# Eighteen first adds of the softmax sums moved to GpSimd, the first batch's factors one place later, one more w_out unit inside the attention

## Chip, cores and metric

One core of one Trainium2 chip runs the whole program. The metric is the device time of one execution in microseconds, over several runs; a profiled execution supplies the trace. TensorE does the matrix products (PE, its weight loads PEld), VectorE (DVE), ScalarE (ACT) and GpSimd (POOL) the rest, and SyncE (SP) starts the DMAs.

## What is computed

Three stages follow each other, each on the output of the one before (B=4 batches, S=448 positions, D=768):

```python
scores = scale * q @ k.transpose            # 4 batches, 12 heads, 448 positions, 64 wide
scores = cap * np.tanh(scores / cap)
attn = softmax(scores) ; x = attn @ v       # heads side by side: (4, 448, 768)

w = softmax of the 2 largest of x @ w_gate  # 4 experts
for e in range(4):                          # causal attention of one head of 64
    out += w[e] * (softmax(mask(q_e @ k_e.T)) @ v_e @ wo[e])

h = gelu(out @ w_in)                        # 768 -> 1024; u, v = halves
v_s = w_sg @ (norm(v) * g_ln) + b_sg        # over positions
y = out + (u * v_s) @ w_out                 # 512 -> 768
```

w_in and w_out arrive as float64 and are split into float32 words in the kernel.

## The kernel before

The attention works on 24 pairs of heads, pair i = 6b + hp (`pairs`), one in each call of `slot(i, side)` (line 281); two more slots empty the pipe. The scores are held transposed, keys on the partitions. Keys 0 to 255 of both heads form the half h = 0, the rest h = 1. `scores(i, h)` (line 201) does the matmuls into PSUM `s`, then tanh (ScalarE, into `p`) and one exponential of the whole half (ScalarE, in place). No maximum is subtracted, since the scores are capped.

The softmax's sum over the keys is made in two steps. `add_up(i, h)` (line 226) adds blocks of keys on VectorE: for h = 0 it makes `pb` (128x896) as the sum of the two blocks of `p`, for h = 1 it adds the third block to `pb`, and in odd slots half a block to each of two `pb`. `sums(b, i)` (line 261) then sums over the partitions with `onehot` on TensorE, for two pairs at once, and VectorE copies or adds the result to `rs`. Its PSUM buffer is from the pool `ps_g`, three buffers that `values` in odd slots and the experts' products use too. Six pairs make a batch. Then `invert(b)` (line 273) takes the reciprocal of `rs`, stores it to DRAM (`rd`) and loads it back, spread over partitions (`rb`, the factors). `values(i)` (line 238) makes the unscaled output `po` from `p` and v (`vv`, `vl`), and `os` holds it in SBUF. `over_sums` (line 331) multiplies `os` by the factors, and `in_parts` (line 335) splits it into a rounded part `xh` and a rest `xl`, the input of the experts.

In slot i the order is: scores(i, 0), side "w", values(i-2), side "a1", the first add, scores(i, 1), side "p", the sums of two pairs in even slots, the second add, side "n". The sides carry other work. In slots 0 to 9 that is the conversion of w_in (`prepare_weights`, on VectorE, products on TensorE); from slot 10 on (`beside`, line 559) a table `PLAN` places the experts' steps of earlier batches, `queries_keys`, `values_chunk`, `gates`, `weigh`, `settle`, `turn`, `attend`. `normed(n, place)` (line 344) places the steps of the factors; its batch is that of slot n - 6. `settle` scales the experts' softmax on GpSimd, `turn` transposes it on TensorE, with copies `pt` by VectorE.

`w_out(k, i, ...)` (line 371) converts one of eight units of w_out: a DMA (`wuw`), six operations of `from64` on VectorE (`wum`), three on GpSimd, two DMAs to DRAM. The table `W_OUT` (line 554) names the slot of each unit; numbers of 26 and more stand for steps of `experts_end` (line 585), which does the rest of the experts after the attention, interleaved with the gMLP of earlier batches (`gsv`, `vg`, the norm).

Up to slot 25, program order is kept on TensorE, VectorE, ScalarE and GpSimd by `InOrder` and `pin` (lines 95 to 120). After that a scheduler orders the instructions by its own costs. The queue of SyncE, which issues the DMAs, is ordered by the scheduler throughout. All operations of VectorE, ScalarE and GpSimd carry line 105 in the profile, all matmuls line 120, transposes line 487.

Of the kernel before, what the change touches and what calls it, by code (L numbers as in the profile page):

```python
# [17 lines left out]
ALU = mybir.AluOpType  # L18
# [4 lines left out]
HP = H // 2  # L23
# [15 lines left out]
def drain(gen):  # L39
    for _ in gen:  # L40
        pass
# [32 lines left out]
def build(ctx: ExitStack, tc: tile.TileContext, a: dict):  # L74
# [4 lines left out]
    def rnd(eng, out, in_):  # L79

        if eng == "a":
            act.activation(out, in_, AF.Copy)
        elif eng == "v":
            dve.tensor_copy(out, in_)
        else:
            pool_e.tensor_scalar(out, in_, 1.0, 0.0, op0=ALU.mult, op1=ALU.add)
# [22 lines left out]
    act, dve, pool_e = InOrder(nc.scalar), InOrder(nc.vector), InOrder(nc.gpsimd)  # L109
# [14 lines left out]
    xp = ES(tc.tile_pool(name="xp", bufs=1, reuse_waits="tile"))  # L124
# [19 lines left out]
    def scale():  # L144
        nc.sync.dma_start(capt, a["cap"].to_broadcast([128, 1]))
        dve.memset(tsc, 0.0)
        act.activation(tsc, tsc, AF.Tanh)
        dve.reciprocal(tsc, capt)
        dve.tensor_scalar(tsc, tsc, 1.0 / math.sqrt(D), None, op0=ALU.mult)
# [25 lines left out]
    at = ah.enter_context(tc.tile_pool(name="at", bufs=2, side="right"))  # L175
# [7 lines left out]
    def load_qk(i):  # L183

        b, hp = pairs[i]
        qk_t[i] = [at.tile([128, S], F32, tag=t, name=f"{t}{i}", bufs=3) for t in ("qp", "kp")]
        nc.sync.dma_start(qk_t[i][1], a["kT"][b, :, hp, :])
        nc.sync.dma_start(qk_t[i][0], a["qT"][b, :, hp, :])

    def load_v(i):  # L190

        b, hp = pairs[i]
        vv = at.tile([128, 2, KT // 128, D], F32, tag="vv", name=f"vv{i}", bufs=3)
        nc.sync.dma_start(vv, a["v"][b, :, 2 * hp:2 * hp + 2])
        vl = None
        if hp % 2:
            vl = at.tile([128, 2, D], F32, tag="vl", name=f"vl{i}", bufs=2)
            nc.sync.dma_start(vl, a["vl"][b, hp // 2])
        v_t[i] = vv, vl

    def scores(i, h):


        last = h == 1 and i % 2 == 1
        n = 2 if h == 0 or last else 1
        p = at.tile([128, 2, n, S], F32, tag=("p0", "p1" if n == 1 else "p2")[h], name=f"p{i}_{h}", bufs=(3, 1)[h])
        pend[i] = (*pend.get(i, ()), p)
        for c2 in range(n):
            s = ps_s.tile([128, 2, 512], F32, tag="s", name=f"s{i}_{2 * h + c2}")
            for j in range(2):  # L210
                r = slice(64 * j, 64 * j + 64)
                if c2 and last:
                    for half in range(2):
                        qp, kp = qk_t[i - 1 + half]
                        mm(s[64 * half:64 * half + 64, j, :S], kp[r, KT:], qp[r, :], start=True, stop=True)
                else:
                    qp, kp = qk_t[i]
                    c = 2 * h + c2
                    mm(s[:, j, :S], kp[r, c * 128:(c + 1) * 128], qp[r, :], start=True, stop=True)
            act.activation(p[:, :, c2, :], s[:, :, :S], AF.Tanh, scale=tsc)  # L220
            yield 805.0


        act.activation(p, p, AF.Exp, scale=capt)

    def add_up(i, h):
        p = pend[i][h]
        if h == 0:
            pb = pbs[i] = at.tile([128, 2, S], F32, tag="pb", name=f"pb{i}", bufs=3)
            dve.tensor_tensor(pb, p[:, :, 0, :], p[:, :, 1, :], op=ALU.add)  # L230
            return
        dve.tensor_tensor(pbs[i], pbs[i], p[:, :, 0, :], op=ALU.add)
        if i % 2:
            for half in range(2):
                r, pb = slice(64 * half, 64 * half + 64), pbs[i - 1 + half]
                dve.tensor_tensor(pb[r], pb[r], p[r, :, 1, :], op=ALU.add)

    def values(i):

        vv, vl = v_t.pop(i)  # L240
        odd = i % 2
        po = po_t[i] = (ps_g if odd else ps_o).tile([128, 512], F32, tag="g" if odd else "po", name=f"po{i}")
        if odd:
            b, hp = pairs[i]
            p = pend[i][1]
            for half in range(2):
                r = slice(64 * half, 64 * half + 64)
                for j in range(2):
                    mm(po_t[i - 1 + half][64 * j:64 * j + 64, :S], vl[r, j, :], p[r, j, 1, :],
                       start=(half == 1), stop=(half == 0))  # L250
            os_t[b, hp // 2] = ao.tile([128, 2, S], F32, tag="os", name=f"os{i}", bufs=4)
            act.activation(os_t[b, hp // 2][:, 0, :], po_t.pop(i - 1)[:, :S], AF.Copy)
        for c in range(KT // 128):
            for j in range(2):
                mm(po[64 * j:64 * j + 64, :S], vv[:, j, c, :], pend[i][c // 2][:, j, c % 2, :],
                   start=(c == 0 and not odd), stop=(c == KT // 128 - 1 and odd == 1))
            yield 805.0
        if odd:
            act.activation(os_t[b, hp // 2][:, 1, :], po_t.pop(i)[:, :S], AF.Copy)
# [21 lines left out]
    def slot(i, side):  # L281

        here = i < len(pairs)
        if i == 0:
            load_qk(0)
            scale()
            load_w(0)
            load_qk(1)  # L290
        if i % 2 == 0 and i + 2 < len(pairs):
            load_qk(i + 2)
        if here:
            first = scores(i, 0)
            drain(islice(first, 2))
            side("a")
            drain(first)
        else:
            side("a")
        side("w")  # L300
        if i > 1:
            drain(values(i - 2))
        if here:
            load_v(i)
        side("a")
        if here:
            add_up(i, 0)
            drain(scores(i, 1))
            if i % 2 == 1 and i + 2 < len(pairs):
                load_qk(i + 2)  # L310
        side("p")
        if 0 < i <= len(pairs):
            b, hp = pairs[i - 1]
            if hp % 2 == 1:
                drain(sums(b, hp // 2))
        if here:
            add_up(i, 1)
        side("n")
# [16 lines left out]
    def in_parts(b, h2):  # L335

        if h2 == 0:
            X[b] = (xp.tile([128, KC, S], F32R, tag="xh", name=f"xh{b}"),
                    xp.tile([128, KC, S], F32R, tag="xl", name=f"xl{b}"))
        (xh, xl), x, o = X[b], os_t.pop((b, h2)), slice(2 * h2, 2 * h2 + 2)  # L340
        rnd("v", xh[:, o, :], x)
        rest("v", xl[:, o, :], x, xh[:, o, :])

    def normed(n, place):

        b = (n - 1) // HP - 1
        step = (n % HP, place)
        if n > B * HP + 4 or b < 0:
            return
        if step == (1, "a1"):  # L350
            invert(b)
        elif step == ((3, "w") if b else (2, "a1")):
            over_sums(b, 0)
            over_sums(b, 1)
            load_rb(b, 2)
        elif b == 0 and step == (3, "w"):
            in_parts(b, 0)
            in_parts(b, 1)
        elif b == 0 and step == (3, "n"):
            over_sums(b, 2)  # L360
            in_parts(b, 2)
        elif b and step == (4, "w"):
            in_parts(b, 0)
            over_sums(b, 2)
        elif b and step == (4, "a1"):
            in_parts(b, 1)
            in_parts(b, 2)
# [159 lines left out]
    def run(works):  # L527
        for b, f, args in works:
            w = f(b, *args)
            if w is not None:  # L530
                yield from w
# [3 lines left out]
    def experts_weights(n, place):  # L535
# [13 lines left out]
        if place == "w" and n in parts:  # L549
# [2 lines left out]


    W_OUT = {11: ("w", xp, "rb0", "rb1"), 14: ("n", at, "ws", "ws"), 17: ("w", at, "ws", "ws"),
             20: ("n", at, "ws", "ws"), 23: ("w", at, "ws", "ws"),
             29: ("n", xp, "rb0", "rb1"), 30: ("n", xp, "rb0", "rb1"), 31: ("n", xp, "rb0", "rb1")}
    ws = {n: w_out(*divmod(u, 2), *W_OUT[n][1:]) for u, n in enumerate(W_OUT)}

    def beside(n):
# [25 lines left out]
    def experts_end(n):  # L585

        for m in range(n, B * HP + 20):
            work = planned(m)
            for place in "asw":
                yield from run(work[place])  # L590
            for place in ("w", "a1"):
                normed(m, place)
            yield from together(run(work["p"]), run(work["t"]), 0.3)
            yield from run(work["n"])
            normed(m, "n")
            if m in W_OUT:
                yield from ws[m]
# [341 lines left out]
```

## Time and profile before

| | us |
|---|---|
| three runs | 569.24, 569.01, 567.21 (median 569.01) |
| the profiled execution, its own time | 565.89 |
| its span, first to last instruction | 564.0 |
| TensorE busy | 524.6 (93% of the span) |
| VectorE busy | 376.3 (67%) |
| ScalarE busy | 304.0 (54%) |
| GpSimd busy | 112.0 (20%) |

The profiled execution is the only one with a trace; 1.9 us of its time lie outside the span. The mean granted clock of TensorE is 0.978 of full speed. A busy share is a mean over stages of different kinds, so what a stage costs is read from its own stretch of the timeline: for TensorE the idle time ahead of an instruction, with the engine and tile that released it, and how long the same matmuls take where the clock is granted at 1.00 (2.4 GHz) or 0.50 (1.2 GHz).

### The profile page before, as it was taken

What the parts mean: (1) busy time and instruction counts of PE and PEld (TensorE: products, weight loads), DVE (VectorE), ACT (ScalarE), POOL (GpSimd) and SP (SyncE); (2) the same over time, 40 slices, a digit from 0 to 9 for tenths busy, and PEclk for the clock granted to TensorE, in tenths of its full rate; (3) what the DMA queues carried; (4) which work ended last, traced back from release to release, by engine and by line L of the source; (5) the groups of instructions that cost most, each with busy time, mean ns of one, the idle gap of its engine ahead of it and who ended that gap; (6) DMA issues with size and microseconds to landing.
All of it is one profiled execution on the core that took longest, in us unless ns stands there. A gap on an engine that the chain in (4) does not pass through costs nothing.

```text
span 564.0 us, 7562 instructions
## 1 busy us (share of the span) xinstructions
PE 524.6 (93%) x2732; PEld 337.1 (60%) x2732; DVE 376.3 (67%) x743; ACT 304.0 (54%) x496; POOL 112.0 (20%) x162
## 2 busy tenths in 40 slices
PE   7999996999889998899998959999999999999997
PEld 2333321445445464556556646877868878889996
DVE  4899999565768856678665589886831787485300
ACT  5886782888566787466722244464534344253211
POOL 0000000020042130140221447614602122031000
PEclk9799997999999999999998988999999999999999
DMA  8954435642505131404115421020232000000111
GB/s 277 335 172 134 156 112 159 194 148 70 166 14 170 46 122 52 129 30 125 35 53 168 104 93 56 16 71 0 86 138 99 2 0 34 33 34 33 50 49 66
DMA packets 32725, 53.99 MB, mean 96 GB/s; under 512 B 4080, under 2 KB 27696, under 8 KB 32688
## 3 DMA queue, kind: packets, MB, share of 16 engines
q1 hardware_dynamic: 31536, 48.27, 27.2%
q0 software_dynamic: 1152, 5.24, 2.7%
q8 instruction: 21, 0.34, 0.3%
q14 instruction: 16, 0.13, 0.1%
HBM read 41.84 MB, written 11.67 MB: 95 GB/s over the span
## 4 chain that ended last, share of the span: by engine, by line
PE 54%; DVE 26%; ACT 6%; DMA 6%; POOL 3%; issue 3%; SPq 0%; DVEq 0%; POOLq 0%; ACTq 0%
PE o L120 14%; DVE pb L105 7%; PE po L120 6%; PE sp L120 5%; PE s L120 5%; PE v L120 5%; PE qk L120 4%; ACT p L105 4%; PE a L120 3%; DMA rb<-rd 3%; PE hv L120 2%; PE hu L120 2%; PE tr L487 2%; DVE rs L105 2%; DVE vg L105 2%
## 5 line engine op out<-in xcount | busy, mean ns | idle before, releaser
L105 ACT ACTIVATE p<-s,tsc 128x896 f32<-128x896 f32 x84 | 81.0, 1004 | 30.9 <-PE s L120 29.9
L120 PE MATMUL s<-qp,kp 64*128 64x448 f32 (+1 forms) x384 | 79.3, 578 | 5.6 <-ACT p L105 5.6
L105 ACT ACTIVATE p<-p,capt 128x1792 f32<-128x1792 f32 (+1 forms) x48 | 77.0, 1604 | 1.3
L120 PE MATMUL po<-p,vv 128*64 128x448 f32 x288 | 61.5, 564 | 0.0
L105 DVE TENSOR_TENSOR pb<-pb,p 128x896 f32<-128x896 f32 (+1 forms) x48 | 51.0, 1084 | 13.5 <-ACT p L105 12.9
L120 PEld LDWEIGHTS s<-qp,kp 64*128 64x128 f32 (+1 forms) x384 | 27.4, 175 | 51.8 <-issue 20.6
L105 POOL TENSOR_SCALAR pe<-pe,cs 112x112 f32<-112x112 f32 (+1 forms) x64 | 35.0, 566 | 94.7 <-DVE cs L105 80.4
L105 ACT ACTIVATE pe<-a,m 112x112 f32<-112x112 f32 (+3 forms) x64 | 31.1, 491 | 27.9 <-DVE m L105 26.8
L105 POOL TENSOR_SCALAR wuw<-wum 128x384 fp32r<-128x384 f32 x8 | 7.0, 872 | 181.2 <-DVE wum L105 173.6
L105 DVE CUSTOM_DVE_ANT_0 a<-a,neg 112x112 f32<-112x112 f32 (+3 forms) x64 | 28.1, 465 | 20.9 <-PE a L120 20.6
L120 PEld LDWEIGHTS po<-p,vv 128*64 128x64 f32 x288 | 19.1, 140 | 36.8 <-issue 35.8
L120 PE MATMUL qk<-xh,wqk_h 128*128 128x448 f32 x96 | 37.8, 394 | 0.9 <-DVE xh L105 0.9
L120 PE MATMUL a<-qk 64*112 64x112 f32 (+3 forms) x128 | 29.4, 433 | 8.9 <-ACT pe L105 6.9
L120 PE MATMUL o<-gh,wu_h 128*128 128x448 f32 x96 | 35.2, 367 | 0.5 <-DMA wu_h<-wud 0.5
L120 PE MATMUL o<-gl,wu_h 128*128 128x448 f32 x96 | 35.4, 369 | 0.0
L120 PE MATMUL qk<-xh,wqk_l 128*128 128x448 f32 x96 | 35.0, 364 | 0.0
L120 PE MATMUL o<-gh,wu_l 128*128 128x448 f32 x96 | 34.8, 367 | 0.0
L487 PE MATMUL tr<-ident,pe 112*112 112x112 f32 x160 | 24.1, 264 | 9.1 <-DVE pt L105 2.4
L105 DVE TENSOR_TENSOR pb<-p 128x896 f32<-128x896 f32 x24 | 27.9, 1162 | 3.8 <-ACT p L105 3.8
L105 ACT ACTIVATE ob<-o 128x448 f32<-128x448 f32 x24 | 12.9, 540 | 31.5 <-PE o L120 31.5
L120 PE MATMUL v<-wvg_h,xh 128*112 128x260 f32 x96 | 29.0, 303 | 0.0
L120 PEld LDWEIGHTS a<-qk 64*112 64x112 f32 x128 | 12.3, 173 | 25.6 <-issue 10.2
(227 smaller groups left out, 1143.1 us busy)
## 6 DMA issues: line engine op xcount, KB each, us to landing
kp<-in_kT_dram SPq DMA_DIRECT2D x24, 224.0 KB, 3.9
qp<-in_qT_dram SPq DMA_DIRECT2D x24, 224.0 KB, 4.1
rb<-rd SPq DMA_DIRECT2D x24, 224.0 KB, 4.7
out_dram<-ob SPq DMA_DIRECT2D x24, 224.0 KB, 1.9
vv<-in_v_dram SPq DMA_DIRECT2D x24, 192.0 KB, 3.0
wuw<-in_w_out_dram SPq DMA_DIRECT2D x8, 384.0 KB, 3.3
wud<-wuw SPq DMA_DIRECT2D x16, 192.0 KB, 1.9
ws<-in_wqk_dram SPq DMA_DIRECT2D x4, 384.0 KB, 5.4
```

Source lines behind the costliest of these rows:

```text
L105: ins = f(*args, **kw)
L120: pin(nc.tensor.matmul(*args, **kw))
L487: pin(nc.tensor.transpose(g[:CP, j * CP:(j + 1) * CP], pe[:, j * CP:(j + 1) * CP], ident))
```

## The change

It has three parts. The first add of a pair moves, for pairs 6 to 23, to GpSimd, and in all slots stands right behind scores(i, 0) instead of behind values(i-2). In the first batch, the multiplications by the factors for two thirds of the heads, with the load of the last factors, move from slot 8's "a1" to its end ("n"), and the second `in_parts` from slot 9's "w" to its "a1". In `W_OUT`, a unit is added at the end of slot 24 and the one of step 30 dropped; the units after it keep their turn, so each does the next words.

```diff
--- before.py
+++ after.py
@@ -227,7 +227,7 @@
         p = pend[i][h]
         if h == 0:
             pb = pbs[i] = at.tile([128, 2, S], F32, tag="pb", name=f"pb{i}", bufs=3)
-            dve.tensor_tensor(pb, p[:, :, 0, :], p[:, :, 1, :], op=ALU.add)
+            (dve if i < HP else pool_e).tensor_tensor(pb, p[:, :, 0, :], p[:, :, 1, :], op=ALU.add)
             return
         dve.tensor_tensor(pbs[i], pbs[i], p[:, :, 0, :], op=ALU.add)
         if i % 2:
@@ -295,6 +295,7 @@
             drain(islice(first, 2))
             side("a")
             drain(first)
+            add_up(i, 0)
         else:
             side("a")
         side("w")
@@ -304,7 +305,6 @@
             load_v(i)
         side("a")
         if here:
-            add_up(i, 0)
             drain(scores(i, 1))
             if i % 2 == 1 and i + 2 < len(pairs):
                 load_qk(i + 2)
@@ -349,12 +349,13 @@
             return
         if step == (1, "a1"):
             invert(b)
-        elif step == ((3, "w") if b else (2, "a1")):
+        elif step == ((3, "w") if b else (2, "n")):
             over_sums(b, 0)
             over_sums(b, 1)
             load_rb(b, 2)
         elif b == 0 and step == (3, "w"):
             in_parts(b, 0)
+        elif b == 0 and step == (3, "a1"):
             in_parts(b, 1)
         elif b == 0 and step == (3, "n"):
             over_sums(b, 2)
@@ -552,8 +553,8 @@
 
 
     W_OUT = {11: ("w", xp, "rb0", "rb1"), 14: ("n", at, "ws", "ws"), 17: ("w", at, "ws", "ws"),
-             20: ("n", at, "ws", "ws"), 23: ("w", at, "ws", "ws"),
-             29: ("n", xp, "rb0", "rb1"), 30: ("n", xp, "rb0", "rb1"), 31: ("n", xp, "rb0", "rb1")}
+             20: ("n", at, "ws", "ws"), 23: ("w", at, "ws", "ws"), 24: ("n", at, "ws", "ws"),
+             29: ("n", xp, "rb0", "rb1"), 31: ("n", xp, "rb0", "rb1")}
     ws = {n: w_out(*divmod(u, 2), *W_OUT[n][1:]) for u, n in enumerate(W_OUT)}
 
     def beside(n):
@@ -588,6 +589,7 @@
             work = planned(m)
             for place in "asw":
                 yield from run(work[place])
+
             for place in ("w", "a1"):
                 normed(m, place)
             yield from together(run(work["p"]), run(work["t"]), 0.3)
```

What it does to the order is shown for three places. The first is VectorE from slot 8 to slot 9, at the end of the w_in conversion (`wqk_l` is a part of the experts' weights, `os1`, `os3` the outputs of the first batch, `pb8` the sums of pair 8). Before:

```order
L105 TENSOR_TENSOR wi11m_639<-wi11m_639,wi11e_640 128x512
L105 TENSOR_TENSOR wqk_l_76<-ws7_564,wqk_h_75 128x6x128
L105 TENSOR_TENSOR os1_306<-os1_306,rb0_0_596 128x896
L105 TENSOR_TENSOR os3_433<-os3_433,rb0_1_599 128x896
L105 TENSOR_TENSOR pb8_666<-p8_0_630 128x896
L105 COPY rs1_681<-sum1_0_676 128x448
L105 TENSOR_TENSOR pb8_666<-pb8_666,p8_1_668 128x896
L105 TENSOR_TENSOR wqk_l_76<-ws8_649,wqk_h_75 128x6x128
```

Now:

```order
L105 TENSOR_TENSOR wi11m_639<-wi11m_639,wi11e_640 128x512
L105 TENSOR_TENSOR wqk_l_76<-ws7_566,wqk_h_75 128x6x128
L105 COPY rs1_676<-sum1_0_671 128x448
L105 TENSOR_TENSOR pb8_649<-pb8_649,p8_1_663 128x896
L105 TENSOR_TENSOR os1_308<-os1_308,rb0_0_598 128x896
L105 TENSOR_TENSOR os3_435<-os3_435,rb0_1_601 128x896
L105 TENSOR_TENSOR wqk_l_76<-ws8_651,wqk_h_75 128x6x128
```

The first add of pair 8 is gone, and the two multiplications stand behind the copy of the sums and the second add instead of ahead of them.

The second place is slot 14, on VectorE (`cs` are the experts' softmax sums, `pt` the copies of the transposes). Before:

```order
L105 RECIPROCAL cs0_0_1_937<-cs0_0_1_937 112x4
L105 TENSOR_TENSOR cs0_0_1_937<-cs0_0_1_937,wt0_1170 112x4
L105 TENSOR_TENSOR pb14_1219<-p14_0_1186 128x896
L105 COPY pt0_0_0_1231<-tr0_0_0_0_1232 112x112
L105 COPY pt0_0_0_1231<-tr0_0_0_1_1235 112x2x112
L105 COPY pt0_0_0_1231<-tr0_0_0_2_1243 112x3x112
```

Now:

```order
L105 RECIPROCAL cs0_0_1_937<-cs0_0_1_937 112x4
L105 TENSOR_TENSOR cs0_0_1_937<-cs0_0_1_937,wt0_1170 112x4
L105 COPY pt0_0_0_1231<-tr0_0_0_0_1232 112x112
L105 COPY pt0_0_0_1231<-tr0_0_0_1_1235 112x2x112
L105 COPY pt0_0_0_1231<-tr0_0_0_2_1243 112x3x112
```

The add of pair 14 no longer stands ahead of the copies. On GpSimd the same place was:

```order
L105 TENSOR_SCALAR pe0_0_1_2_1054<-pe0_0_1_2_1054,cs0_0_1_937 112x336
L105 TENSOR_SCALAR pe0_0_1_3_1086<-pe0_0_1_3_1086,cs0_0_1_937 112x448
L105 TENSOR_SCALAR wuw0_1_1179<-wum0_1_1180 128x384
L105 TENSOR_TENSOR wum0_1_1180<-wum0_1_1180,wuw0_1_1179 128x384
```

and is now:

```order
L105 TENSOR_SCALAR pe0_0_1_2_1054<-pe0_0_1_2_1054,cs0_0_1_937 112x336
L105 TENSOR_SCALAR pe0_0_1_3_1088<-pe0_0_1_3_1088,cs0_0_1_937 112x448
L105 TENSOR_TENSOR pb14_1210<-p14_0_1186 128x896
L105 TENSOR_SCALAR wuw0_1_1179<-wum0_1_1180 128x384
L105 TENSOR_TENSOR wum0_1_1180<-wum0_1_1180,wuw0_1_1179 128x384
L105 TENSOR_TENSOR wuw0_1_1179<-wum0_1_1180 128x384
L105 TENSOR_TENSOR pb15_1296<-p15_0_1286 128x896
```

The add of pair 14 comes behind the scalings of `settle` and ahead of the w_out unit, that of pair 15 behind it.

The third place is VectorE in the last batch after slot 25, where the scheduler orders (`os23` is the last output of the attention, `gsv` and `vg` with the BN rows the norm of the gMLP's first tiles, `wum` a w_out unit, `xh3` and `xl3` the last batch's parts). Before:

```order
L105 TENSOR_TENSOR os23_2441<-os23_2441,rb3_2_2707 128x896
L105 SCALAR_TENSOR_TENSOR vg0_0_2662<-gsv0_0_2663,hv0_0_2627 112x512
L105 BN_STATS bs0_0_2669<-vg0_0_2662 112x6
L105 BN_AGGR mv0_0_2671<-bs0_0_2669 112x2
L105 TENSOR_SCALAR rstd0_0_2673<-mv0_0_2671 112x1
L105 TENSOR_SCALAR wum2_1_2974<-wuw2_1_2973 128x384
L105 TENSOR_SCALAR wum2_1_2974<-wum2_1_2974 128x384 x2
L105 TENSOR_TENSOR gsv0_1_2724<-gsv0_1_2724,hv0_1_2679 112x512
L105 SCALAR_TENSOR_TENSOR wum2_1_2974<-wuw2_1_2973,wum2_1_2974 128x384
L105 TENSOR_SCALAR wum2_1_2974<-wum2_1_2974 128x384
L105 SCALAR_TENSOR_TENSOR wum2_1_2974<-wuw2_1_2973,wum2_1_2974 128x384
L105 CAST xh3_2834<-os19_2031 128x896
```

Now:

```order
L105 TENSOR_TENSOR os23_2455<-os23_2455,rb3_2_2721 128x896
L105 TENSOR_SCALAR wum3_0_2988<-wuw3_0_2987 128x384
L105 TENSOR_TENSOR gsv0_0_2677<-gsv0_0_2677,hv0_0_2641 112x512
L105 TENSOR_SCALAR wum3_0_2988<-wum3_0_2988 128x384 x2
L105 SCALAR_TENSOR_TENSOR wum3_0_2988<-wuw3_0_2987,wum3_0_2988 128x384
L105 SCALAR_TENSOR_TENSOR vg0_0_2676<-gsv0_0_2677,hv0_0_2641 112x512
L105 TENSOR_SCALAR wum3_0_2988<-wum3_0_2988 128x384
L105 BN_STATS bs0_0_2683<-vg0_0_2676 112x6
L105 SCALAR_TENSOR_TENSOR wum3_0_2988<-wuw3_0_2987,wum3_0_2988 128x384
L105 CAST xh3_2848<-os19_2033 128x896
L105 CAST xh3_2848<-os21_2248 128x896
L105 CAST xh3_2848<-os23_2455 128x896
```

The w_out unit that comes here begins ahead of the norm of the first tile, `vg0_0` and its BN rows stand between its operations, and BN_AGGR comes after the casts.

## Rows read from the trace of the kernel before

**Rows 1.** The page: busy us, share of the span and instructions of each engine.

```profile
PE 524.6 (93%) x2732; PEld 337.1 (60%) x2732; DVE 376.3 (67%) x743; ACT 304.0 (54%) x496; POOL 112.0 (20%) x162
```

**Rows 2.** Windows: length, busy us (instructions) per engine, TensorE's granted clock, DMA share, GB/s.

```profile
40.00:80.00 40.00, 40.00 (x184) 13.34 (x178) 38.64 (x60) 31.36 (x31) 0.00 (x0) 1.00 0.47 152
...
92.50:98.50 6.00, 5.91 (x16) 1.53 (x16) 5.93 (x8) 0.00 (x0) 0.00 (x0) 0.50 0.42 129
150.00:162.00 12.00, 8.32 (x46) 4.81 (x43) 8.35 (x26) 5.74 (x6) 4.65 (x8) 1.00 0.38 93
...
335.00:341.00 6.00, 3.77 (x12) 1.53 (x14) 5.45 (x15) 1.21 (x6) 2.87 (x3) 0.50 0.35 104
```

**Rows 3.** Timeline of TensorE, 69 to 99 us: start, us, operation, count [idle before, releaser].

```profile
69.12 2.48 PE L120 MATMUL po<-p,vv 128*64 128x448 f32 x12
...
83.03 0.95 PE L120 MATMUL sum<-pb,onehot 128*32 128x448 f32 x4 [0.68 <-DVE pb L105]
84.16 0.95 PE L120 MATMUL sum<-pb,onehot 128*32 128x448 f32 x4 [0.17 <-DVE pb L105]
...
92.59 1.76 PE L120 MATMUL po<-p,vl 64*64 64x448 f32 x4 [4.89 <-DVE rs L105]
94.28 4.75 PE L120 MATMUL po<-p,vv 128*64 128x448 f32 x12
```

**Rows 4.** Timeline of VectorE, 79 to 93 us, same columns.

```profile
79.76 1.03 DVE L105 TENSOR_TENSOR pb<-p 128x896 f32<-128x896 f32 x1
...
88.92 2.08 DVE L105 TENSOR_TENSOR os<-os,rb 128x896 f32<-128x896 f32 x2
90.92 1.08 DVE L105 TENSOR_TENSOR pb<-p 128x896 f32<-128x896 f32 x1
91.92 0.62 DVE L105 COPY rs<-sum 128x448 f32<-128x448 f32 x1
```

**Rows 5.** Timelines of VectorE and TensorE, 323 to 369 us, the experts' last batch.

```profile
323.14 0.69 DVE L105 BATCH_NORM_STATS2 bs<-vg 112x6 f32<-112x512 f32 x1
...
325.69 0.36 DVE L105 TENSOR_SCALAR wum<-wuw 128x384 int32<-128x384 int32 x1 [1.45 <-DMA wuw<-in_w_out_dram]
...
336.31 0.27 DVE L105 CUSTOM_DVE_ANT_0 a<-a,neg 112x112 f32<-112x112 f32 x1
...
337.23 1.08 PE L120 MATMUL a<-qk 64*112 64x224 f32 x2 [5.41 <-ACT pe L105]
...
368.33 0.63 PE L120 MATMUL a<-qk 64*112 64x224 f32 x2 [1.17 <-ACT pe L105]
```

**Rows 6.** Timelines of VectorE and TensorE in slots 14 and 19.

```profile
157.79 1.25 DVE L105 TENSOR_TENSOR pb<-p 128x896 f32<-128x896 f32 x1 [1.58 <-ACT p L105]
158.96 0.56 DVE L105 COPY pt<-tr 112x112 f32<-112x112 f32 x2
...
159.37 0.47 PE L487 MATMUL tr<-ident,pe 112*112 112x112 f32 x3 [1.45 <-POOL pe L105]
...
226.21 0.47 PE L487 MATMUL tr<-ident,pe 112*112 112x112 f32 x3 [2.05 <-DVE pt L105]
```

**Rows 7.** Timelines of GpSimd and VectorE where they meet, 332 to 340 us.

```profile
332.44 2.00 POOL L105 TENSOR_TENSOR sg_l<-w_sgT,sg_h 112x448 fp32r<-112x448 f32 x1
...
333.35 2.04 DVE L105 TENSOR_TENSOR xl<-os,xh 128x896 fp32r<-128x896 f32 x1
...
338.83 1.14 POOL L105 TENSOR_TENSOR sg_l<-w_sgT,sg_h 112x448 fp32r<-112x448 f32 x1
```

**Rows 8.** Timelines of ScalarE, VectorE and TensorE in slot 10.

```profile
107.72 1.79 ACT L105 ACTIVATE p<-p,capt 128x1792 f32<-128x1792 f32 x1
...
110.15 0.63 DVE L105 CAST xh<-os 128x896 fp32r<-128x896 f32 x1
...
111.24 0.36 PE L120 MATMUL qk<-xh,wqk_h 128*128 128x448 f32 x1
```

**Rows 9.** Tile wum, from64's two-input operations: shortest/median/longest ns, first to last start.

```profile
L105 DVE SCALAR_TENSOR_TENSOR wum<-wuw,wum x16: 551/559/1534, 118.0 to 359.9; 128x384 int32<-128x384 int32 x8, 128x384 f32<-128x384 uint32 x8
```

## The prediction

> **What bounds the kernel now.** I read the page's busy times first: TensorE is busy for 524.6 of 564.0 us and VectorE for 376.3 [rows 1]. So time can go in three ways only: TensorE's idle stretches (here mostly under a microsecond or two), the stretches in which its clock is at the lower of its two levels, 1.2 instead of 2.4 GHz, and what a change opens anew. I then took the 40 us windows: from 40 to 80 us TensorE is busy for all 40.00 us, and VectorE for 38.64 in the same time [rows 2]. Attention there hides the conversion of w_in, but VectorE has next to no slack, so a thing put on it or in its way moves everything behind it.
>
> The timelines of TensorE and VectorE around 80 to 100 us give the largest stall of the first half. The sums' matmuls wait 0.68 and 0.17 us for VectorE's second add; then the PV matmuls stand still for 4.89 us until VectorE's copy of the sums (`rs`) frees the PSUM buffer [rows 3]. Ahead of that copy VectorE does two multiplications of batch 0 (2.08 us) and the first add of pair 8 (1.08) [rows 4]. The stall costs twice: the granted clock is 0.50 from 92.5 to 98.5 us [rows 2], and twelve PV matmuls that took 2.48 us at 69.12 take 4.75 [rows 3]. The second stall of this size is at 331.82 to 337.23, 5.41 us, in the last batch of the experts, again with a window at 0.50 behind it [rows 2, 5].
>
> **The change, part by part.**
>
> *The add on GpSimd.* Eighteen adds of 128x896 leave VectorE, where one takes 1.03 to 1.25 us [rows 4, 6]. GpSimd does not run this shape in the trace before. Its nearest row is an add-like operation of two SBUF inputs with 448 columns: 1.14 us undisturbed, 2.00 where it met VectorE [rows 7]. Twice the columns give an estimate of 2.1 to 2.3 us. What matters more is what such an instruction does to VectorE: the subtraction `xl` that ran beside it took 2.04 us, where 1.08 is usual for an operation of that shape [rows 4, 7], so VectorE stood for 0.96 us of GpSimd's 1.14. Operations of VectorE with one input, or with one in PSUM, show no such delay. Per 896 columns I take a hold of 1.9 us on VectorE's two-input operations (2 x 0.96). The bounds are 0 (VectorE's operations slip in ahead, or have one input) and 3.8 (the add takes twice as long as the row implies).
>
> The Trainium skill, "SBUF — State Buffer", section "Who interferes with whom", says that the two engines' shared port pair is an exclusive lock, that a VectorE instruction with two SBUF inputs contends for it with a GpSimd instruction that reads SBUF, and that the loser is blocked for the whole instruction. The trace agrees nearly: 0.96 of 1.14 us. By the rule the hold would be the add's whole 2.1 to 2.3 us, and the sum below about 0.6 us worse; it speaks against moving an add beside a VectorE that is full.
>
> *Slots 6 to 8.* In slots 6 and 7 VectorE has no slack, so each add saves 1.05 us and holds 1.9. The sums' matmuls of 83.03 and 84.16 come 2 x 0.85 = about 1.6 us later, and their gaps of 0.68 and 0.17 grow to about 2.4 together. The copy `rs` at 91.92 loses what stood ahead of it, 88.92 to 91.92, which is 3.0 us, and gains the 1.6: it runs at about 90.56 and ends at 91.2. PV resumes at 91.2 instead of 92.59: **-1.4 us**. The second gap is then about 1.9 us instead of 4.89. I take it that the clock stays up, since it does elsewhere beside waits of this size: in the window from 150 to 162 us TensorE is busy for 8.32 of 12 us, and the granted clock is 1.00 [rows 2]. Then the twelve PV matmuls gain 4.75 - 2.48 = 2.27, and the four before them 1.76 x 2.27/4.75 = 0.84: **-3.1 us**.
>
> *Slot 10.* The batch's factors are no longer ahead of `xh`; its last third still is. The first qk matmul that needs it is at 111.24, just after the cast `xh` of 110.15 to 110.78; 4.5 us earlier it would be due at 106.74. The exponential of slot 10 ends at 109.51, that is 105.0 when moved [rows 8]; GpSimd's add starts there. The multiplication `os` (half of 2.08) has the port until 105.6, the add holds until 107.5, `xh` follows until 108.1. So qk waits 1.4 us: **+1.4**. Slots 6 to 10 together: **-3.1 us**, between -5.5 (nothing of the holds counts) and +1 (the clock falls as before and the adds hold longer).
>
> *The later slots.* In slot 14 the first add of the pair waits for its exponential and runs 157.79 to 159.04, with two copies `pt` behind it; TensorE's transposes wait 1.45 us until the first of these has freed a PSUM buffer at 159.24 (the row names GpSimd's scaling, whose third result, the one needed, was there some 2 us before) [rows 6]. With the add away the copies run at once: **-1.45**. On GpSimd it stands behind the eight scalings there; its pair's sums come two slots later, which covers it. In slot 19 the first add stands ahead of the copies for which transposes wait 2.05 us [rows 6]: **-1.03**, an add's time [rows 4]. Elsewhere the adds that leave VectorE lie in waits for exponentials, and those that come run beside PSUM-reading or idle stretches: 0, and where that cover is gone one hold of 1.9 each, in slots 16 and 22 above all, where `xh` leads straight to qk. Sum: -2.5 us (0 to -2.5 from the rows; -2.5 taken since both waits have VectorE's queue behind them).
>
> *The unit of w_out.* A unit is four VectorE operations of 0.36 and two of 0.56 us, 2.6 in all [rows 5, 9], three on GpSimd, one DMA in and two out. One moves from the experts' part to slot 24; the SP queue has no wait on it there that TensorE sees, and VectorE pays the 2.6 us in a slot whose end it mostly idles through: 0.4 us. But behind slot 25 the scheduler sets the order anew, and the unit that now comes first stands ahead of the norm of the gMLP's first tile. That norm (three operations of 0.69, rounded to 2.1 us) was done before 325.69, during VectorE's 1.45 us wait for the w_out words [rows 5]; now it follows that wait, ahead of `xl`, which leads to the mask `a` at 336.31 and TensorE's 337.23. I take 2.25, with the 0.4 **+2.65 us**, and 0.8 more from half clock (the window 335 to 341 at 0.50 grows with the stall by a third of 2.65, rounded) [rows 2]. One unit less follows in the experts' part, where a similar wait is 1.17 us [rows 5]: -1.0. Sum: **+2.4 us**, between 0 (the norm slips in as before) and +5 (both w_out and the norm whole, nothing returned).
>
> *The sum.* -3.1 - 2.5 + 2.4 = -3.2 us. On the profiled execution's own time of 565.9 us that is 562.7. The median of the runs is 569.0, 3.1 us above this execution, so the median comes to 565.8, and I forecast **566.0**.
>
> **The rivals.** A run-to-run measurement tells about 0.5% here, 2.85 us.
>
> *The costs do not come* (chance 0.25): VectorE's operations slip in between, so slots 6 to 10 give -5.5, the later slots -2.5, and the last batch nothing: 561.0. For it: the stall at 92 us has a clear cause that the change takes away. Against: VectorE is full in 40 to 80 us.
>
> *The clock still falls* (0.18): two gaps of 2.4 and 1.9 us within nine microseconds together do what one of 4.89 did. The 3.1 us stay, and so does the 1.4 us of slot 10, since qk then is 1.4 early and waits for nothing: -1.4 - 2.5 + 2.4 = -1.5, 567.5. For it: TensorE is stopped for 4.3 us of nine, against 5.7 before. Against: the window at 150 us [rows 2].
>
> *The add on GpSimd takes twice as long* (0.15): 4.2 us, a hold of 3.8. Slots 6 and 7 lose 1.9 more each, PV resumes at 95.0 with the clock down (+2.4 for slots 6 to 8), `xh` in slots 16 and 22 comes 1.9 later each (+3.8): 2.4 + 3.8 - 2.5 + 2.4 = +6.1, **575.1**, slower. It decides from a hold of 3.0 us on: four holds lie on the path, and -1.5 + 4 x (hold - 1.9) passes 2.85 there. For it: GpSimd's 448 columns took 2.00 us when they met VectorE [rows 7]. Against: the time in that row is a wait, not work.
>
> That the change does not do what it says is excluded by the order: all eighteen adds stand on GpSimd.
>
> **How the numbers follow.** The forecast has 0.42 (564 to 568 us), a little over half of it beyond the 2.85 us. Faster by over 0.5%: 0.23 + 0.25 = 0.48. Within: 0.19 of the forecast less 0.01, and 0.18: 0.36. Slower: 0.15 + 0.01 = 0.16. The range reaches from just below the first rival to half-way to the last, 560.5 to 571.5, which leaves out most of the last rival and the tails.
>
> **What would show it.** Right: GpSimd's `pb` rows near 2.2 us; VectorE's second adds in slots 6 and 7 near 2.9 us for what they met; a gap of about 1.9 us before PV near 91 us, and a granted clock of 1.00 from there to 99; no stall of transposes in slot 14; the stall at 332 us longer, near 8. Wrong: a window at 0.50 between 85 and 99 us, or gaps over 1 us before qk in slots 16 and 22. If the stall at 332 us is unchanged or shorter, the last batch's term has failed; if `pb` on GpSimd takes over 3 us, the last rival holds.

## The result and the profile after

The changed kernel took **569.69 us** (median of 20 runs, 567.81 to 573.47), the kernel before 566.67 us over 20 runs (563.81 to 569.24): a ratio of **1.006**, 95% interval 1.0043 to 1.0078, so 2.4 to 4.4 us slower. The forecast was 566.0 against a median of 569.0 for before, 3 us faster; the sign was wrong, and more runs moved the median of before down by 2.3 us, so ratios are the better measure from here on.

The profiled execution has a span of 566.0 us, before 564.0. The page of the changed kernel and its windows, to set beside [rows 1, 2]:

```profile
PE 523.6 (93%) x2732; PEld 340.2 (60%) x2732; DVE 358.2 (63%) x725; ACT 303.7 (54%) x496; POOL 145.9 (26%) x180
```

```profile
85.00:99.00 14.00, 11.90 (x53) 3.70 (x54) 13.71 (x17) 7.67 (x8) 2.50 (x1) 1.00 0.47 130
148.00:160.00 12.00, 9.77 (x56) 5.64 (x56) 7.21 (x26) 6.29 (x7) 5.91 (x9) 1.00 0.33 89
344.00:354.00 10.00, 6.54 (x17) 4.34 (x17) 9.10 (x21) 4.99 (x11) 7.10 (x8) 0.66 0.11 39
```

VectorE lost 18.1 us of work and TensorE does the same work, yet the end is later. In this execution the attention did about what was forecast. TensorE's timeline, to set beside [rows 3, 6]:

```profile
68.38 0.97 PE L120 MATMUL po<-p,vl 64*64 64x448 f32 x4 [1.00 <-DVE rs L105]
...
85.05 0.94 PE L120 MATMUL sum<-pb,onehot 128*32 128x448 f32 x4 [2.54 <-DVE pb L105]
86.17 0.94 PE L120 MATMUL sum<-pb,onehot 128*32 128x448 f32 x4 [0.17 <-DVE pb L105]
...
91.59 0.97 PE L120 MATMUL po<-p,vl 64*64 64x448 f32 x4 [1.88 <-DVE rs L105]
92.49 2.48 PE L120 MATMUL po<-p,vv 128*64 128x448 f32 x12
...
220.61 0.47 PE L488 MATMUL tr<-ident,pe 112*112 112x112 f32 x3 [1.05 <-DVE pt L105]
```

The gap before PV is 1.88 us instead of 4.89, the clock stays at 1.00 from 85 to 99 us, and the twelve PV matmuls take 2.48 instead of 4.75. In slot 14 no transpose waits any more, in slot 19 1.05 instead of 2.05. When slot 23's exponential ends, the changed kernel is 6.0 us ahead; 1.4 of these were there by slot 4 and are not the change's (this execution of before had a granted clock of 0.51 from 13.5 to 20 us, where the changed one had 1.00; a second profile of the changed kernel is 0.5 us behind before at slot 4).

Then the lead goes, in two steps. The matmuls `a` are the scores of the experts' attention, which VectorE masks and ScalarE takes the exponential of. VectorE and TensorE before, in the last batch, where the forecast has [rows 5]:

```profile
300.45 2.95 DVE L105 RECIPROCAL rs<-rs 128x448 f32<-128x448 f32 x1
314.83 1.09 DVE L105 TENSOR_TENSOR os<-os,rb 128x896 f32<-128x896 f32 x1 [2.38 <-DMA rb<-rd]
...
345.61 0.82 PE L120 MATMUL a<-qk 64*112 64x336 f32 x2
...
350.50 1.00 PE L120 MATMUL a<-qk 64*112 64x448 f32 x2 [0.48 <-ACT qk L105]
```

And of the changed kernel:

```profile
294.98 2.95 DVE L105 RECIPROCAL rs<-rs 128x448 f32<-128x448 f32 x1
313.67 1.09 DVE L105 TENSOR_TENSOR os<-os,rb 128x896 f32<-128x896 f32 x1 [5.25 <-DMA rb<-rd]
...
324.34 0.36 DVE L105 TENSOR_SCALAR wum<-wuw 128x384 int32<-128x384 int32 x1 [3.12 <-DMA wuw<-in_w_out_dram]
...
332.44 0.65 PE L120 MATMUL a<-qk 64*112 64x224 f32 x2 [2.47 <-ACT pt L105]
335.20 1.08 PE L120 MATMUL a<-qk 64*112 64x224 f32 x2 [2.11 <-ACT pe L105]
...
341.51 0.36 DVE L105 TENSOR_SCALAR wum<-wuw 128x384 int32<-128x384 int32 x1 [6.33 <-DMA wuw<-in_w_out_dram]
...
345.65 0.82 PE L120 MATMUL a<-qk 64*112 64x336 f32 x2 [1.76 <-ACT pe L105]
348.28 1.46 PE L120 MATMUL a<-qk 64*112 64x336 f32 x2 [1.81 <-ACT y L105]
353.99 1.00 PE L120 MATMUL a<-qk 64*112 64x448 f32 x2
```

The reciprocal of the last batch's sums is 5.5 us ahead of before, the first multiplication by the factors only 1.2: 4.3 us are lost between the two. The matmuls `a` of 224 columns that end the stall come at 335.20 instead of 337.23 [rows 5], so 2.0 us of the lead are left there; the next, of 336 columns, are level at 345.6, those of 448 columns 3.5 us behind. Later 1.5 us come back, where one w_out unit less is left, and the span ends 2.0 us longer.

For the first step, the queue of SyncE, before and then changed:

```profile
276.88 3.38 SPq L384 DMA_DIRECT2D wud<-wuw  x2
280.31 1.84 SPq L721 DMA_DIRECT2D w_sgT<-in_w_sgT_dram  x4
303.42 0.34 SPq L276 DMA_DIRECT2D rd<-rs  x1
```

```profile
292.30 2.49 SPq L385 DMA_DIRECT2D wud<-wuw  x2
294.84 1.99 SPq L723 DMA_DIRECT2D w_sgT<-in_w_sgT_dram  x4
297.96 0.34 SPq L276 DMA_DIRECT2D rd<-rs  x1
```

The unit of slot 24 puts its two stores (`wud`) into this queue; they wait for GpSimd until 292.3, and the four loads of w_sg behind them, 784 KB, start at 294.8 instead of 280.3, just ahead of the store `rd` of the sums. The DMA view (KB each, us to landing), before and changed:

```profile
w_sgT<-in_w_sgT_dram SPq DMA_DIRECT2D x4, 196.0 KB, 3.3
rd<-rs SPq DMA_DIRECT2D x1, 224.0 KB, 5.1
```

```profile
w_sgT<-in_w_sgT_dram SPq DMA_DIRECT2D x4, 196.0 KB, 9.2
rd<-rs SPq DMA_DIRECT2D x1, 224.0 KB, 10.2
```

The second step is on VectorE: 6.33 us of waiting for the words of the next w_out unit, with the mask of the matmuls `a` queued behind it.

### The profile page after: what moved, and what is told of

It reads as the page before. It is cut to its first block, busy times and chain, and to the rows that moved or that the text cites. A ratio compares the mean times of both kernels' runs of the same rounds, so it can differ in the third digit from the quotient of the medians.

```text
span 566.0 us, 7564 instructions
## 1 busy us (share of the span) xinstructions
PE 523.6 (93%) x2732; PEld 340.2 (60%) x2732; DVE 358.2 (63%) x725; ACT 303.7 (54%) x496; POOL 145.9 (26%) x180
## 4 chain that ended last, share of the span: by engine, by line
PE 63%; DVE 16%; DMA 7%; ACT 7%; issue 3%; POOL 2%; SPq 1%; DVEq 0%; POOLq 0%; ACTq 0%
PE o L120 14%; PE s L120 8%; PE po L120 7%; PE sp L120 7%; PE qk L120 6%; PE v L120 5%; ACT p L105 4%; PE a L120 3%; DVE pb L105 3%; PE hu L120 3%; PE w2ps L120 2%; PE hv L120 2%; PE tr L488 2%; DMA qp<-in_qT_dram 2%; DMA rd<-rs 2%
## 5 line engine op out<-in xcount | busy, mean ns | idle before, releaser
L120 PE MATMUL s<-qp,kp 64*128 64x448 f32 (+1 forms) x384 | 77.7, 564 | 7.4 <-ACT p L105 6.0
L105 POOL TENSOR_TENSOR pb<-p 128x896 f32<-128x896 f32 x18 | 38.7, 2151 | 163.6 <-ACT p L105 152.6
L105 DVE TENSOR_TENSOR pb<-pb,p 128x896 f32<-128x896 f32 (+1 forms) x48 | 54.0, 1146 | 15.3 <-ACT p L105 10.2
L120 PE MATMUL po<-p,vv 128*64 128x448 f32 x288 | 59.3, 546 | 0.0
L105 POOL TENSOR_SCALAR pe<-pe,cs 112x112 f32<-112x112 f32 (+1 forms) x64 | 31.9, 519 | 75.7 <-DVE cs L105 75.6
L120 PE MATMUL a<-qk 64*112 64x112 f32 (+3 forms) x128 | 31.0, 439 | 10.0 <-ACT pe L105 5.0
L120 PE MATMUL v<-wvg_h,xl 128*112 128x260 f32 x96 | 27.6, 288 | 0.0
```

What stands on the lines that cost most here:

```text
L105: ins = f(*args, **kw)
L120: pin(nc.tensor.matmul(*args, **kw))
```

## The experiments

All ratios are against the kernel before, run beside them on the same chip; a gain or loss in us is taken from the ratio, unless two medians are named.

**Which part costs, and which gains.** Units back:

```diff
-             20: ("n", at, "ws", "ws"), 23: ("w", at, "ws", "ws"), 24: ("n", at, "ws", "ws"),
-             29: ("n", xp, "rb0", "rb1"), 31: ("n", xp, "rb0", "rb1")}
+             20: ("n", at, "ws", "ws"), 23: ("w", at, "ws", "ws"),
+             29: ("n", xp, "rb0", "rb1"), 30: ("n", xp, "rb0", "rb1"), 31: ("n", xp, "rb0", "rb1")}
```

> The changed kernel with the w_out units at their old places (step 30 again, nothing at slot 24). Theory A (the unit in slot 24 costs the time: its stores stand ahead of the w_sgT loads in SyncE's queue, those 784 KB then land beside the store rd of the factors, and the last batch starts late): rd lands in about 5 us instead of 10.2, the last batch loses nothing, and the 4.6 us that the attention gained (6.0 at slot 23 in the profile, less 1.4 that were there before slot 5) stay: 562 us, 561 to 563.5. Theory B (the last batch absorbs whatever the attention gains, since it waits for the factors' DMAs and w_out words anyway): 566 to 567.

Measured: 561.39 us, ratio 0.991 (0.9877 to 0.9944); `rd` landed in 2.5 us, half of what was expected. The unit alone, the same lines the other way round in the kernel before:

> The kernel before with only the w_out unit moved to slot 24. Theory A: the whole loss of the last batch shows without the other parts: rd lands in about 10 us, and the time is 6 to 8 us above before, 572.5 to 574.5. Theory B: the unit alone costs at most the 2.4 us of the prediction: 566 to 569.

Measured: 571.47 us, ratio 1.0099 (1.0062 to 1.0136), 5.6 us slower, a little under the expected 6 to 8; `rd` landed in 9.4 us. So the other two parts are worth 5 us, and the one w_out unit costs more than that: 5.6 us in the kernel before, and in the changed one 1.006 against 0.991, some 8.5 us.

The factors alone in the kernel before:

```diff
-        elif step == ((3, "w") if b else (2, "a1")):
+        elif step == ((3, "w") if b else (2, "n")):
...
+        elif b == 0 and step == (3, "a1"):
             in_parts(b, 1)
```

> The kernel before with only the first batch's factors one place later. The two multiplications (2.08 us) leave from ahead of the copy rs in slot 8, so the gap before PV should fall from 4.89 to about 2.8 us. Theory A (the stall at 92 us is set by VectorE's queue, and the gain of the attention is mostly this): 2.1 us and some of the 3.1 us of half clock, less up to 1.2 for xh in slot 10: 562 to 565. Rival (the gain comes from the adds alone): 565.5 to 566.5.

Measured: 563.77 us, ratio 0.9963 (0.9935 to 0.9991), 2.1 us faster, as theory A had it; the gap before PV was 2.88 us. The adds alone in the kernel before:

```diff
-            dve.tensor_tensor(pb, p[:, :, 0, :], p[:, :, 1, :], op=ALU.add)
+            (dve if i < HP else pool_e).tensor_tensor(pb, p[:, :, 0, :], p[:, :, 1, :], op=ALU.add)
...
             drain(first)
+            add_up(i, 0)
...
-            add_up(i, 0)
             drain(scores(i, 1))
```

> The kernel before with only the first adds on GpSimd, at their new place. Theory A: slots 6 and 7 lose about 1.7 us to the holds and 1.0 before PV of slot 6, the gap at slot 8 stays near 5 us with half clock; slots 14, 16, 19 and 22 gain 3.4 us, and w_h and w_l are issued some 5 us earlier against rd than before, so that rd lands in about 2.5 us instead of 5.1 and the factors of the last batch come 2 us earlier: 562 to 565. Rival (the holds eat what the adds give): 566 or more.

Measured: 565.38 us, ratio 0.9972 (0.9945 to 0.9999), 1.6 us faster, with an interval that ends just below 1; the median lies just above the expected range. `rd` landed in 2.5 us, as expected, and the gap in slot 8 was 3.88 us, not near 5. Both parts gain; 2.1 and 1.6 against 5.1 together leave 1.4 us, which the intervals allow.

**Place or engine of the add.** With units back and the adds on VectorE again, at the new place:

```diff
-            (dve if i < HP else pool_e).tensor_tensor(pb, p[:, :, 0, :], p[:, :, 1, :], op=ALU.add)
+            dve.tensor_tensor(pb, p[:, :, 0, :], p[:, :, 1, :], op=ALU.add)
```

> The changed kernel with the w_out units at their old places and the first adds back on VectorE (still right behind the first scores); left of the change are the first batch's later factors. If the add on GpSimd is worth what the attention's profile suggests (slots 14, 19, 22: 3.4 us, less what its holds cost in slots 6, 7 and 10), this is 1 to 3 us slower than the kernel with units back, 563 to 565, and transposes in slot 14 wait 1 us or more again. If the later factors alone carry the gain, the two are equal within 0.5 us. Copy rs before PV in slot 8 should come without the 3 us of multiplications: a gap of 2 to 3 us instead of 4.89, clock 1.00.

Measured: 578.86 us, ratio 1.022 (1.0178 to 1.0262). A miss by 14 us, and not an undoing: behind scores(i, 0) the add makes VectorE wait for the exponential with the sides' work queued behind it. TensorE loses little by little over slots 12 to 23 (its longest waits there are 2.99 us at 150.9 and, at 293.6, 3.56). So the new place was worth having only with the add on GpSimd, which idles there. The reverse, GpSimd's add at the old place:

```diff
             drain(first)
-            add_up(i, 0)
...
         if here:
+            add_up(i, 0)
             drain(scores(i, 1))
```

> The changed kernel with the w_out units at their old places and the adds on GpSimd, but each first add at its old place in program order, behind values(i-2). If the new place only matters for VectorE (578.9 us with the adds on it there), GpSimd's adds start at the same times and this equals the kernel with units back: 561 to 562. Rival: the new place also changes the order in which the pool's buffers are laid out, which frees the room of w_h and w_l earlier; then w_h waits here for the last PV again, rd lands in about 5 us, and the time is 563 to 564.5.

Measured: 564.23 us, ratio 0.9968 (0.9943 to 0.9992), against 0.991 with the new place: the rival, with intervals that just touch. GpSimd's loads of the gMLP's weights, in this kernel and then in the one with units back:

```profile
295.18 1.30 POOL L716 DMA_DIRECT2D w_h<-w2d  x2 [7.83 <-PE po L120]
296.46 1.09 POOL L717 DMA_DIRECT2D w_l<-w2d  x2
```

```profile
293.23 1.29 POOL L716 DMA_DIRECT2D w_h<-w2d  x2 [3.74 <-PE sum L120]
297.32 1.05 POOL L717 DMA_DIRECT2D w_l<-w2d  x2 [2.79 <-PE po L120]
```

At the new place the first load waits for the sums' matmuls instead of the last PV, and so leaves the way of `rd` earlier: 2.5 us to landing instead of 5.4. That the order of allocation moved the buffers under w_h is the reading of these releasers, not shown by itself. Nor is it shown that the whole difference of the two ratios comes from this: `rd` began at 299.94 in the first of these profiles and at 302.08 in the second, so it landed only 0.8 us earlier there.

**Why the unit costs.** First the transfers: the w_sg loads held behind the factors' loads, with the unit left in slot 24.

```diff
-            nc.sync.dma_start(t, a["w_sgT"][:, k, :])
+            d = nc.sync.dma_start(t, a["w_sgT"][:, k, :])
+            tc.add_manual_dep(d.ins, rb_ins[3, 1, 1].ins.name,
...
```

> The changed kernel with the four w_sgT loads held in SyncE's queue behind the factors' loads rb of the last batch's first two thirds; the unit stays in slot 24. Theory A: rd lands in 5 to 6 us, the factors come 4 to 5 us earlier, and the time falls to 562 to 565. Rival (what costs is VectorE's or GpSimd's work for the unit or the scheduler's order, not the transfers): rd may land sooner, but the time stays above 568.

Measured: 565.59 us, ratio 0.999 (0.9961 to 1.0019), with `rd` at 6.6 us: half of the loss is gone, a little less than theory A had. The loads of w_sg are not all that delays `rd`, which took 2.5 us with the units back. On GpSimd the unit's three operations (291.76 to 294.44 in the changed kernel) stand ahead of the issue of `w_h` and `w_l`, 2 MB. With the w_sg loads held, the last of these began at 296.79, 2.3 us ahead of `rd`; with the units back 4.8 us ahead of it (297.32 and 302.08). That this is the rest of the delay is argued from these times alone. But the scheduler also put the norm ahead of the w_out unit again, so this did not separate transfers from order. The next run did: the changed kernel with a rule for the scheduler alone, that the first w_out unit after the attention begins on VectorE only behind the norm (a dependence without a wait of its own, of that unit's first operation on the norm's `rstd`).

```diff
+        if (k, i) == (3, 0):
+            marks["wum"] = marks["words"]
+            norm_first()
...
+            if (b, c) == (0, 0):
+                marks["rstd"] = r
+                norm_first()
```

> The changed kernel with one rule more for the scheduler: the first w_out unit after the attention may begin on VectorE only behind the norm of the gMLP's first tile; it then comes among the operations xl. The DMAs stay as they are in the changed kernel, so rd should still land in about 10 us. Theory C (of the 8 us that the unit in slot 24 costs, some 5 are the late factors and 2 to 3 the new order, in which the words' wait stands ahead of the norm): the wait of 3.1 us ahead of xh goes, and the time falls by 2 to 3 us, to 566.5 to 568. Rival (the order is worth nothing, since the words' unit then only comes later and its wait moves on to the next mask): 569 to 571.

> The changed kernel itself, for comparison beside the one above: 569.7 us, within 1 us, rd landing in about 10 us, the wait for w_out words of 6 us near 341 us.

Measured: 561.65 us with the rule, ratio 0.9928 (0.9901 to 0.9955); 570.4 us without, ratio 1.007 (1.0047 to 1.0093). 8.75 us between these medians (8.0 by the ratios) from the order, three times what was expected, and **the transfers stayed as late**: DMA view and VectorE's timeline of the kernel with the rule.

```profile
w_sgT<-in_w_sgT_dram SPq DMA_DIRECT2D x4, 196.0 KB, 8.2
rd<-rs SPq DMA_DIRECT2D x1, 224.0 KB, 9.4
```

```profile
320.15 1.47 DVE L105 TENSOR_TENSOR os<-os,rb 128x896 f32<-128x896 f32 x1 [2.79 <-DMA rb<-rd]
...
325.81 1.49 DVE L105 CAST xh<-os 128x896 fp32r<-128x896 f32 x2
327.82 0.34 DVE L105 TENSOR_SCALAR wum<-wuw 128x384 int32<-128x384 int32 x1
...
328.69 3.08 DVE L105 TENSOR_TENSOR xl<-os,xh 128x896 fp32r<-128x896 f32 x3
...
348.13 0.35 DVE L105 TENSOR_SCALAR wum<-wuw 128x384 int32<-128x384 int32 x1
```

The last `os` comes at 320.15, as in the changed kernel (320.05), but VectorE waits for no words: neither 3.12 us at 324 nor 6.33 at 341. The rule moved other work as well (rows on TensorE, ScalarE and GpSimd changed places), so the 8.75 us belong to the whole order that follows from it; the two waits are what the traces show gone. The matmuls `a` of 224 and of 448 columns on TensorE, with the rule and then in the second profile of the changed kernel, taken beside it:

```profile
332.88 1.08 PE L120 MATMUL a<-qk 64*112 64x224 f32 x2 [1.54 <-ACT pe L105]
346.01 1.00 PE L120 MATMUL a<-qk 64*112 64x448 f32 x2
```

```profile
337.28 1.08 PE L120 MATMUL a<-qk 64*112 64x224 f32 x2 [2.13 <-ACT pe L105]
356.39 1.00 PE L120 MATMUL a<-qk 64*112 64x448 f32 x2
```

The kernel with the rule was 1.1 us ahead when slot 23's exponential ended, 4.4 at the first of these and 10.4 at the second: 3.3 us came from the stretch of the first wait, 6.0 from that of the second.

**The place of the unit.** The six units of the attention at slots 11, 14, 16, 18, 20 and 22, then the same with the first later unit held behind `xl`, and the kernel before with only that second rule:

```diff
+    W_OUT = {11: ("w", xp, "rb0", "rb1"), 14: ("n", at, "ws", "ws"), 16: ("n", at, "ws", "ws"),
+             18: ("n", at, "ws", "ws"), 20: ("n", at, "ws", "ws"), 22: ("n", at, "ws", "ws"),
+             29: ("n", xp, "rb0", "rb1"), 31: ("n", xp, "rb0", "rb1")}
```

> The changed kernel with its six w_out units of the attention at slots 11, 14, 16, 18, 20 and 22 instead of 11, 14, 17, 20, 23 and 24: as many units in the attention, but the last one's stores leave the queue before the w_sgT loads. Theory A (it is the place of the unit, late in SyncE's queue and GpSimd's, not the unit): rd lands in 2 to 4 us, and with one unit less behind the attention the time is 559.5 to 562. Rival (any sixth unit costs, by VectorE's 2.6 us or by the order of the last batch): 564 or more.

> The changed kernel with its sixth unit in slot 22 (slots 11, 14, 16, 18, 20, 22), and the first w_out unit after the attention held on VectorE behind the last batch's xl. Theory D (a w_out unit ahead of xh and xl on VectorE is what costs in the last batch, since its words arrive only after the factors): the stall before the matmuls a near 330 us shrinks by about 3 us against the kernel with the unit in slot 22 alone (561.8 us): 557.5 to 560. Rival (the unit moved behind only waits and blocks elsewhere, as its stores then hold the next words): 561 to 563.

> The kernel before with nothing but the same rule: the first w_out unit after the attention held on VectorE behind the last batch's xl. Theory D: the unit's 3.1 us with its wait leave from ahead of xh, the stall of 5.41 us at 332 us shrinks to 1 to 2.5 us, and the time falls by 3 to 5 us, to 561.5 to 563.5. Rival (before, the order cost nothing; it only matters with the unit in slot 24): 565.5 to 567.

Measured: 561.83 us, ratio 0.993 (0.9906 to 0.9954); 560.59 us, ratio **0.9884** (0.9856 to 0.9912), the best of all and 6.6 us under the kernel before; and 564.54 us, ratio 0.9966 (0.994 to 0.9992). Within these intervals a sixth unit in the attention thus costs no more than one behind it, where its stores leave the queue in time. The rule's own gain was smaller than expected: 1.9 us in the kernel before (3 to 5 were expected), where the stall at 332 us did fall from 5.41 to 2.72 us; about 1 us with the unit in slot 22, within the intervals, and there the stall did not shrink as theory D had it: it was 2.73 us with the rule and 1.57 without.

## Why the prediction was wrong

**VectorE's holds: right in the sum, wrong in what was held.** GpSimd's adds took 2.15 us in the mean (2.1 to 2.3 was the estimate). Pair 8's add ran from 80.96 to 83.04, and VectorE's second add of pair 7, begun at 81.74, took until 84.00, 2.25 us instead of 1.09. That is what the Trainium skill's page "SBUF — State Buffer" says in "Who interferes with whom": blocked to the end of the other's instruction. The sums' gaps came to 2.54 + 0.17 us (2.4 forecast), the gap before PV to 1.88 (1.9), the wait of qk in slot 10 to 1.22 (1.4).

That they came out so is in part luck. The sum had two holds of 1.9 us ahead of the sums' matmuls, both on second adds. The trace has three, of 1.8, 1.8 and 1.2 us: pair 6's add held the half-block adds of pair 5 (4.00 us for two, 2.20 before), pair 7's add held an operation of the w_in conversion with one input, and pair 8's the one above. VectorE in the changed kernel (two operations, 0.89 us together before, beside GpSimd's add of 69.58 to 71.67; then the second add), and at last a row of the kernel before:

```profile
69.70 2.72 DVE L105 TENSOR_SCALAR wi9m<-wi9m 128x512 f32<-128x512 f32 x2
81.74 2.25 DVE L105 TENSOR_TENSOR pb<-pb,p 128x896 f32<-128x896 f32 x1
```

```profile
345.36 1.21 DVE L105 TENSOR_SCALAR vg<-vg,mv,rstd 112x512 f32<-112x512 f32 x1
```

So the prediction misread the trace of before when it said that operations with one input show no such delay: this one has one tensor as input, met GpSimd's operation of 345.29 to 346.29, and took 1.21 us, where the same operation takes 0.55 at 350.08.

**The clock at 92 us: right in half of the profiles.** The granted clock was 1.00 from 85 to 99 us in the changed kernel's profile, but in that of the kernel with units back, with gaps of 2.54 and 1.87 us in the same places, it was 0.76 over the same stretch:

```profile
85.00:99.00 14.00, 11.95 (x44) 3.14 (x48) 13.73 (x17) 4.67 (x5) 2.49 (x1) 0.76 0.46 131
```

It is 0.88 in a second profile of the changed kernel. Of the eight profiles with the adds on GpSimd and the later factors, four have 1.00 there, three 0.88 and one 0.76. So the forecast and the rival of the falling clock both happen, from execution to execution; that this profile had the 3.1 us was luck.

**Slots 6 to 10: right in sign, too large.** From slot 6 to slot 11 the profiles give 1.4 us, where 3.1 were forecast: pair 6's add also holds VectorE ahead of the addition to `rs` in slot 6, and PV waits 1.00 us at 67.4, which the sum did not have. The second profile of the changed kernel gives 2.3, and that of the kernel with units back a loss of 1.7, with the clock of 0.76 above. **The later slots:** 3.4 us gained, where 2.5 were forecast; slots 14 and 19 as named, the rest near slots 16 and 22. This too depends on the execution: the second profile gives 1.8. No transpose waits in its slot 14 either, but its granted clock is 0.72 from 156 to 160 us, where the first has 1.00.

**The unit of w_out: the step that failed.** The prediction said that "the SP queue has no wait on it there that TensorE sees". It has: the unit's stores wait for GpSimd there, and 784 KB behind them move into the landing time of `rd`, 10.2 us instead of 5.1. That was not among the costs at all. And the term of +2.65 us for the new order was read from one wait, the stall at 332 us, which was to grow to near 8. It got shorter, 2.47 and 2.11 us with two matmuls between them instead of 5.41; by the prediction's own sign the term had failed. From the last `os` to `xh` VectorE took 7.2 us instead of 6.3, 0.9 more where 2.25 were taken, and the three `xl` then took 3.09 us, where they had taken 4.86 beside GpSimd. Late factors make this wait for words late too: the words go into a buffer (`rb0`) that the factors leave, and their load started at 321.25, as the last `os` ended. The dearer wait was the next one: a w_out unit in VectorE's queue waits for words whose load is issued only when the stores of the unit before have left that buffer, and those wait for GpSimd, whose operation on `wum` took 3.90 us beside VectorE's `xl` (0.99 to 1.73 elsewhere):

```profile
331.24 3.90 POOL L105 TENSOR_TENSOR wum<-wum,wuw 128x384 f32<-128x384 f32 x1
```

So the next unit came 6.33 us late, with a mask behind it, two more gaps on TensorE (1.76 and 1.81 us), and a clock of 0.66 from 344 to 354 us. The part was put at +2.4 us, with +5 as its bound; the lead fell by 8.0 us in the profile, and the runs give some 8.5. The rival that was given for a slower kernel, an add of over 3 us, was not what happened.

**Which of the two decides.** In the changed kernel, with the factors as late as ever, the order gives back all of the loss that the intervals can tell (0.9928, against 0.991 with the units back). Late factors cost by what is queued behind them. The kernel before with the unit alone shows it the other way round: there `vg` and the first BN row of the norm stood ahead of the unit, but the scheduler had put the multiplications `os` ahead of the gates' operations, so `cs` waited with them, and the transposes with `cs` (VectorE's, then TensorE's timeline of that kernel):

```profile
319.64 1.09 DVE L105 TENSOR_TENSOR os<-os,rb 128x896 f32<-128x896 f32 x1 [7.61 <-DMA rb<-rd]
320.65 0.21 DVE L105 TENSOR_REDUCE rank<-gt 112x16 f32<-112x64 f32 x1
...
327.40 0.23 DVE L105 TENSOR_TENSOR cs<-cs,wt 112x4 f32<-112x4 f32 x2
```

```profile
328.07 1.06 PE L487 MATMUL tr<-ident,pe 112*112 112x112 f32 x3 [5.50 <-POOL pe L105]
```

What stays open is how much of the 8.75 us the two waits for words account for by themselves; no run took away one of them and kept the rest of the order.

## What to carry to other kernels

When a step with DMAs is moved, list what stands behind each of its DMAs in the issuing queue and what those will then collide with; a store that waits for an engine is a wait for all loads behind it. Where a scheduler orders by its own costs, one step moved can reorder the stretch after it: look there for operations that wait for a DMA ahead of the work on the path, and pin that order, which was worth more here (8.75 us) than the whole gain of the change (5 us).

## What was not expected of the hardware

A cast of 128x896 from SBUF to SBUF, with one input, was held too. VectorE's and GpSimd's timelines of the changed kernel in slot 10, first VectorE:

```profile
106.10 2.42 DVE L105 CAST xh<-os 128x896 fp32r<-128x896 f32 x1
```

```profile
105.53 2.49 POOL L105 TENSOR_TENSOR pb<-p 128x896 f32<-128x896 f32 x1 [11.05 <-PE s L120]
```

It took 2.42 us instead of 0.63 [rows 8] and ended 0.5 us after the add, whereas the prediction said that operations with one input show no such delay (its sum for slot 10 let this cast wait all the same). The Trainium skill, "SBUF — State Buffer", "Who interferes with whom", has this case: VectorE in a two-port mode contends with GpSimd. The trace shows the hold, and not the mode. The reciprocal from 78.88 to 81.82, one input too, ran its usual 2.94 us beside GpSimd's add of 80.96.
